# Three of VectorE's routing operations of a group of tokens folded into others

## The chip, the cores and the metric

The kernel runs on one core of one Trainium2 chip. The core's engines each follow their own list of instructions and wait for each other at semaphores: TensorE (PE, matmuls; PEld is its loading of weights), VectorE (DVE), ScalarE (ACT), GpSimd (POOL) and SyncE (SP, which here only issues transfers). 16 DMA engines move data between the main memory (HBM) and the on-chip memory (SBUF). Matmul results land in eight PSUM banks. The metric is the device time of one execution in microseconds, lower is better.

## The reference

Attention in chunks of 64 keys is followed by a mixture of experts in which each of 4608 tokens goes to one of 16 experts, picked in two steps (one of 4 groups by the largest of 4 logits, then one of the group's 4 experts):

```python
scores = scale * np.matmul(q_c, k_c.transpose(0, 1, 2, 4, 3))
scores = scores - np.max(scores, axis=-1, keepdims=True)
attn = np.exp(scores)
attn = attn / (np.sum(attn, axis=-1, keepdims=True) + 1e-09)
out = np.matmul(attn, v_c)
...
g_logits = x @ w_group
g_idx = np.argmax(g_logits, axis=1)
g_sm = softmax_of(g_logits)          # exp(l - max) / (sum + 1e-09)
g_w = g_sm[np.arange(N), g_idx]
for g in range(G):
    xg = x[g_idx == g]
    e_logits = xg @ w_expert[g]
    e_idx = np.argmax(e_logits, axis=1)
    e_w = the same softmax's value at e_idx
    for e in range(Eg):
        h = np.maximum(xg[e_idx == e] @ w1[g, e], 0.0)
        ye = h @ w2[g, e]
        out[those tokens] = (g_w * e_w)[:, None] * ye
```

`softmax_of` and the last lines are shortened here. B, H, S, D = 8, 8, 576, 64, so x has 4608 rows of 512, and each expert has F = 1024. All data is fp32.

## The kernel before

The 4608 tokens are 36 tiles of 128 (one token in each partition). An attention phase goes over the tiles in a software pipeline. In step t, SyncE loads queries, keys (`qk`) and values (`va`) ahead; TensorE makes the scores of tile t+1 (`stage_b`, L578); VectorE takes the maximum and subtracts it (`stage_sub`: `m` L586, `pr` L590); ScalarE exponentiates (`pr` L596); TensorE transposes (L602), ScalarE copies to `pT` (L604), TensorE multiplies by the values (L615); VectorE divides by the sums (`stage_norm`: `rc` L622 and L624, `x` L633); TensorE transposes `x` (L645), ScalarE copies it to `xT` (L646), and TensorE makes the router's logits (L665, L672), which ScalarE copies to `lg` (L673).

Four tiles are a group, so there are nine groups, 0 to 8. `route(g)` is VectorE's work on a group's 4 x 5 sets of 4 logits (one set over groups, four over the experts of each group): the maximum `mx` (L702), where it is (`one` L707), the differences `ls` (L709), the place of the maximum with ties going to the first (L713, L719, L721), the one-hot of 16 experts per token `oh` (L725), sums of the exponentials `sm` (L735; ScalarE exponentiates `ls` into `ex`, L691), the chosen group's sum (L738, L740), the added 1e-9 (L743), the reciprocal (L747), and the product, which is the token's weight (L750). `cum[:, g + 1]` is, by partition, how many tokens of groups 0 to g went to each expert: the sum of the group's four one-hots (L746) plus the count before (L748). `stage_e3(g)` turns counts and one-hots into each token's rank among its expert's tokens by matmuls (L763 to L768), `place(g)` and `one_scatter` turn that into row numbers (`pos`, L785 and L810), and GpSimd scatters the tokens' rows to those rows of `xs` in HBM (L801).

A Recorder takes all these instructions down in the order in which the code runs, works out the semaphore waits from the memory that each one reads and writes, and then plays each engine's list. `route` is a generator: each `yield` is a place where VectorE's list takes up attention work again (`more(n)` resumes it n times), so the two are interleaved by hand and each engine executes its list in order. The last tiles and the first steps of the first expert follow one string, TAIL. Then a loop over units of 128 or 256 tokens of one expert runs on TensorE with loaded weights (L1144, L1159), while VectorE and ScalarE split the next expert's fp32 weights into two parts. SBUF tiles are laid out one behind the other: the tile `cum` stands ahead of the weights' and the queries' buffers.

Of the kernel before, what the change touches and what calls it, by code (L numbers as in the profile page):

```python
# [10 lines left out]
F32 = mybir.dt.float32  # L11
F32R = mybir.dt.float32r
BF16 = mybir.dt.bfloat16
I32 = mybir.dt.int32
AF = mybir.ActivationFunctionType
ALU = mybir.AluOpType
AX = mybir.AxisListType
# [3 lines left out]
P = 128  # L21
# [7 lines left out]
E = G * EG  # L29
NT = N // P  # L30
NG = 4
RPE = N // P
NG0 = NT // NG
# [329 lines left out]
def moe_kernel(tc, qk, v, wgs, w1, w2, cst, out):  # L363
    nc = tc.nc
# [3 lines left out]
    with ExitStack() as ctx:  # L368
# [17 lines left out]
        cum = wpool.tile([P, NG0 + 1, E], BF16, name="cum")  # L386
# [96 lines left out]
        with ExitStack() as c1:  # L483
# [42 lines left out]
            R.vector.memset(cum[:, 0, :], 0.0)  # L526
# [165 lines left out]

            def route(g):
# [12 lines left out]
                one = rpool.tile([P, R5, 4], F32, name="one")  # L706
                V.tensor_tensor(out=by_t(one), in0=L, in1=by_t(mb), op=ALU.is_equal)  # L707
# [4 lines left out]
                io = cs[:, C_IOTA4:C_IOTA4 + 4].unsqueeze(1).broadcast_to([P, R5, 4])  # L712
                V.scalar_tensor_tensor(out=one, in0=one, scalar=-64.0, in1=io, op0=ALU.mult, op1=ALU.add)  # L713
                ex = rpool.tile([P, R5, 4], F32, name="ex")
                st["ex"] = ex, ls
# [8 lines left out]
                oh = rpool.tile([P, NG, 4, 4], BF16, name="oh")  # L724
# [7 lines left out]
                for i in range(NG):  # L732
# [6 lines left out]
                    elif i == 2:  # L739
                        V.tensor_reduce(out=sv[:, :, 1], in_=se, axis=AX.X, op=ALU.add)  # L740
                    else:
                        gt = rpool.tile([P, NG, 2], F32, name="gt")
                        V.tensor_scalar(out=gt, in0=sv[:, :, 0:2], scalar1=1e-9, scalar2=None, op0=ALU.add)  # L743
                    yield
                with nc.allow_low_precision(reason="a sum of four ones and zeros"):
                    V.tensor_reduce(out=cum[:, g + 1, :], in_=oh.rearrange("p t g e -> p (g e) t"), axis=AX.X, op=ALU.add)  # L746
                V.reciprocal(gt, gt)  # L747
                V.tensor_tensor(out=cum[:, g + 1, :], in0=cum[:, g + 1, :], in1=cum[:, g, :], op=ALU.add)  # L748
# [6 lines left out]
            def stage_e3(g):  # L755
# [8 lines left out]
                R.tensor.matmul(rk3, lhsT=ones, rhs=wide(cum[:, g, :], NG), start=False, stop=False)  # L764
# [5 lines left out]
                if g == GC:  # L770
                    n = rk[0:1, NG * E:NG * E + E]
                    R.tensor.matmul(n, lhsT=ones[:, 0:1], rhs=cum[:, g + 1, :], start=True, stop=True)
# [244 lines left out]
        with tc.tile_critical():  # L1017
            with nc.Block() as blk, nc.allow_low_precision(reason="sums of a whole number or of four ones, and zeros"):

                @blk.tensor  # L1020
                def _(pe):
# [163 lines left out]
                    pe.matmul(pxf[0][0:E, 0:1], lhsT=cum[:, NG0, :], rhs=ones[:, 0:1], start=False, stop=True).then_inc(S["TP"], 1)  # L1185
# [536 lines left out]
```

## Time and profile before

| | |
|---|---|
| three timed runs | 613.26, 613.39, 618.44 us (median 613.39) |
| the profiled execution, and its span | 618.42 us, 616.8 us |
| attention phase | to about 158 us of the span |
| busy in the span: PE, DVE, ACT, POOL | 579.8, 360.8, 263.3, 158.2 us |

The span runs from the first to the last instruction; 1.6 us of the execution lie outside it. The busy time of VectorE is spread over two phases that have different limits, so the profile is read by stretches of time.

### The profile page before, as it was taken

The page shows a single profiled execution, that of the slowest core. Times are in us where ns is not written, and L with a number is a line of the kernel's source. Part 1 is how long each engine was busy: PE and PEld are TensorE (multiplying, and loading weights), DVE is VectorE, ACT ScalarE, POOL GpSimd, SP SyncE. Part 2 cuts the span into 40 slices and gives each one's busy share as a digit, 9 for nine tenths or more (in the row PEclk, how much of TensorE's full clock was granted, in tenths as well). Part 3 has the DMA queues.
Part 4 walks back from the last instruction along what each step waited for, and adds up shares of the span by engine and source line. Part 5 has one row for each costly group of instructions (what it writes and reads, how often), then busy time and mean ns, then how long its engine had stood idle before and what let it go on. Part 6 is the DMA issues. An engine that isn't in the chain of part 4 may idle for free.

```text
span 616.8 us, 16000 instructions
## 1 busy us (share of the span) xinstructions
PE 579.8 (94%) x5711; PEld 498.9 (81%) x5712; DVE 360.8 (58%) x688; ACT 263.3 (43%) x367; POOL 158.2 (26%) x252
## 2 busy tenths in 40 slices
PE   7889979978998999999999999999999999999995
PEld 4666657756887989888889989889989988898984
DVE  4577869776767482136697474726326578763211
ACT  2455545756336241223685252626116355452111
POOL 0002314665403111212323312122111124321120
PEclk9899889997998999999999999999999999999999
DMA  7998997876549693118298763643613586921110
GB/s 280 422 312 277 352 366 240 243 228 207 163 146 395 240 330 109 39 30 296 103 348 311 261 245 121 221 153 113 236 51 123 208 323 223 331 105 64 34 44 24
DMA packets 43104, 128.27 MB, mean 208 GB/s; under 512 B 4590, under 2 KB 4974, under 8 KB 41136
## 3 DMA queue, kind: packets, MB, share of 16 engines
q1 hardware_dynamic: 32192, 93.93, 43.9%
q0 software_dynamic: 10864, 33.64, 15.5%
q8 instruction: 37, 0.61, 0.4%
q14 instruction: 11, 0.09, 0.1%
HBM read 106.40 MB, written 21.93 MB: 208 GB/s over the span
## 4 chain that ended last, share of the span: by engine, by line
PE 71%; DVE 11%; DMA 7%; issue 5%; POOL 2%; SPq 1%; ACT 1%; another core or an unknown queue 0%; DVEq 0%; POOLq 0%; ACTq 0%
PE banks L1159 28%; PE banks L1144 22%; PE banks L1128 4%; PE banks L615 2%; DVE x L633 2%; DVE pr L590 2%; DMA xgr<-xs 2%; DVE m L586 2%; DMA w1r<-in_moe_w_dram 2%; DMA qk<-in_qk_dram 2%; PE banks L471 2%; PE banks L602 2%; PE banks L1044 2%; PE banks L645 1%; PE banks L578 1%
## 5 line engine op out<-in xcount | busy, mean ns | idle before, releaser
L1144 PE MATMUL banks<-big,w1h 128*128 128x256 f32 x896 | 128.1, 283 | 1.4 <-issue 1.4
L1144 PEld LDWEIGHTS banks<-big,w1h 128*128 128x128 f32 x896 | 117.3, 192 | 2.9 <-issue 1.9
L1305 ACT ACTIVATE big<-banks 128x512 fp32r<-128x512 f32 x58 | 34.5, 596 | 158.9 <-PE banks L1144 126.0
L1159 PE MATMUL banks<-big,big 128*128 128x512 f32 x360 | 84.7, 393 | 0.0
L1635 POOL DMA_INDIRECT out_dram<-xl,io__154 x37 | 41.1, 1112 | 152.9 <-DVE xl L1371 144.4
L1159 PEld LDWEIGHTS banks<-big,big 128*128 128x128 f32 x360 | 66.5, 188 | 14.4 <-ACT big L1355 0.7
L1404 DVE SCALAR_TENSOR_TENSOR big<-banks,big 128x512 fp32r<-128x512 f32 x54 | 36.1, 687 | 64.3 <-ACT big L1305 62.0
L1159 PE MATMUL banks<-w2h,big 128*128 128x512 f32 x288 | 72.6, 399 | 0.2 <-ACT big L1305 0.2
L1144 PE MATMUL banks<-big,w1l 128*128 128x256 f32 x448 | 72.3, 283 | 0.6 <-DVE w1l L1381 0.6
L1381 DVE TENSOR_TENSOR w1l<-w1r,w1h 128x2048 fp32r<-128x2048 f32 x28 | 63.1, 2291 | 16.0 <-ACT w1h L1292 14.3
L1371 DVE TENSOR_SCALAR xl<-banks,io__154 128x512 f32<-128x512 f32 x33 | 24.7, 749 | 68.2 <-PE banks L1159 68.2
L1159 PEld LDWEIGHTS banks<-w2h,big 128*128 128x128 f32 x288 | 53.8, 190 | 12.2 <-ACT big L1305 0.9
L1144 PEld LDWEIGHTS banks<-big,w1l 128*128 128x128 f32 x448 | 61.9, 192 | 0.8 <-DVE w1l L1381 0.8
L1292 ACT CAST w1h<-w1r 128x2048 fp32r<-128x2048 f32 x28 | 52.2, 1903 | 7.8 <-DMA w1r<-in_moe_w_dram 6.0
L578 PE MATMUL banks<-qk 64*64 64x64 f32 x1152 | 27.8, 232 | 12.5 <-DMA qk<-in_qk_dram 3.5
L578 PEld LDWEIGHTS banks<-qk 64*64 64x64 f32 x1152 | 22.3, 141 | 20.8 <-DVE pr L590 4.5
L1385 DVE TENSOR_TENSOR w2l<-w2r,w2h 128x1024 fp32r<-128x1024 f32 x32 | 37.1, 1220 | 2.3 <-ACT w2h L1324 1.7
L1159 PE MATMUL banks<-w2l,big 128*128 128x512 f32 x144 | 35.6, 389 | 0.0
L604 ACT COPY pT<-banks 128x512 f32<-128x512 f32 x36 | 21.1, 586 | 33.6 <-PE banks L602 30.2
L615 PEld LDWEIGHTS banks<-va,pT 64*64 64x64 f32 x1152 | 21.4, 141 | 16.5 <-issue 4.8
L801 POOL DMA_INDIRECT xs<-x,pos x24 | 24.2, 1008 | 40.3 <-DVE pos L810 21.7
L1629 POOL COPY in__155<-xgr 128x2 int32<-128x2 int32 x22 | 10.7, 485 | 92.6 <-PE banks L1044 78.7
(223 smaller groups left out, 906.8 us busy)
## 6 DMA issues: line engine op xcount, KB each, us to landing
w1r<-in_moe_w_dram SPq DMA_DIRECT2D x30, 1024.0 KB
w2r<-in_moe_w_dram SPq DMA_DIRECT2D x30, 1024.0 KB
qk<-in_qk_dram SPq DMA_DIRECT2D x15, 1024.0 KB, 17.4
xgr<-xs POOLq DMA_DIRECT2D x38, 257.0 KB, 5.6
va<-in_v_dram SPq DMA_DIRECT2D x24, 390.0 KB
qk<-in_qk_dram SPq DMA_DIRECT2D x6, 512.0 KB, 8.7
w1r<-in_moe_w_dram POOLq DMA_DIRECT2D x2, 1024.0 KB, 9.4
w2r<-in_moe_w_dram POOLq DMA_DIRECT2D x2, 1024.0 KB, 8.2
```

The lines of the kernel that those rows point to most:

```text
L578: R.tensor.matmul(sc[cols, x, hp * CH:hp * CH + CH], lhsT=T[rows, 0, hp, cols], rhs=T[rows, 1, hp, cols], start=True, stop=True)
L615: R.tensor.matmul(o[cols, x, hp * W:hp * W + W], lhsT=pT[rows, hp, cols], rhs=v_at(2 * t + c)[rows, hp], start=True, stop=True)
L1128: m = pe.matmul(ph[n], a_[:, c, 0:P], w_[:, c, n * 512:(n + 1) * 512], start=(i == 0), stop=(i == 11))
L1144: m = pe.matmul(ph[f // 2][:, f % 2 * 256:f % 2 * 256 + 256], w_[:, c, f * P:(f + 1) * P], a_[:, c, :], start=(i == 0), stop=(i == 11))
L1159: m = pe.matmul(py[j], a_[:, f, half[j]], w_(b, f), start=(i == 0), stop=(i == 23))
L1292: lambda b, s, j: ac.copy(wt[b][0][:, s], w1r[j]), K1)
L1305: ac.activation(hth()[:, 2 * b:2 * b + 2, :], ph[b].rearrange("p (f t) -> p f t", f=2), AF.Relu).then_inc(S["Ha"], 1)
L1371: return ve.tensor_scalar(out=yb[:, j, :], in0=py[j], scalar1=io_[:, j, 1:2], scalar2=None, op0=ALU.mult)
L1381: lambda b, s, j: ve.tensor_sub(wt[b][1][:, s], w1r[j], wt[b][0][:, s].bitcast(F32)), K1, js)
L1385: m = ve.tensor_sub(wt[b][4 + 2 * j + i], w2r[j][:, 2 * i:2 * i + 2], wt[b][2 + j][:, 2 * i:2 * i + 2].bitcast(F32))
L1404: ve.scalar_tensor_tensor(out=htl()[:, 2 * b:2 * b + 2, :], in0=ph[b].rearrange("p (f t) -> p f t", f=2), scalar=0.0, in1=hth()[:, 2 * b:2 ...
L1635: gp.indirect_dma_start(out, bass.IndirectOffsetOnAxis(ap=io[:, j, 0:1].bitcast(I32), axis=0), yb[:, j, :], None, bounds_check=N - 1, oob_ ...
```

## The change

It takes three instructions of `route` out of VectorE's list for each of nine groups.

1. The place of the maximum. Before, one instruction marked where a logit equals the maximum and a second made of this -64 + index there and the index elsewhere. Now the second reads the differences `ls` directly: (ls == 0) times (index - 64), which is -64 + index at the maximum and 0 elsewhere.
2. The added 1e-9. `ex` has a fifth column that holds 1e-9 from the start, so the sum over five has it; the reciprocal reads the sum directly.
3. The running counts. Three tiles `ohs` of 5 x 16 take turns: row 0 is the count before the group, rows 1 to 4 are its one-hots. One sum over the five rows writes row 0 of the next tile. TensorE reads the counts there.

Two memsets of 128x20 are added at the program's start; the one that cleared `cum` now clears row 0 of the first tile. The three tiles take 480 bytes per partition where `cum` took 320, and so all tiles allocated behind them start 160 bytes further on.

```diff
@@ -383,7 +383,7 @@
         pos8 = wpool.tile([P, NG], I32, name="pos8")
-        cum = wpool.tile([P, NG0 + 1, E], BF16, name="cum")
+        ohs = [wpool.tile([P, NG + 1, E], BF16, name="oh%d" % i) for i in range(3)]
         ones = wpool.tile([P, P], BF16, name="ones")
...
@@ -523,7 +523,6 @@
             R.vector.memset(off[:, E:E1], 2.0 * P)
-            R.vector.memset(cum[:, 0, :], 0.0)
             wg = cpool.tile([P, 4, 32], F32, name="wg")
...
@@ -690,6 +689,11 @@
 
+            exs = [cpool.tile([P, 5 * NG, 5], F32, name="ex%d" % i) for i in range(2)]
+            for z in exs:
+                R.vector.memset(z[:, :, 4:5], 1e-9)
+            R.vector.memset(ohs[0][:, 0], 0.0)
+
             def route(g):
...
@@ -703,16 +707,15 @@
                 by_t = lambda z: z.rearrange("p (t r) j -> p t r j", r=5)
-                one = rpool.tile([P, R5, 4], F32, name="one")
-                V.tensor_tensor(out=by_t(one), in0=L, in1=by_t(mb), op=ALU.is_equal)
                 ls = rpool.tile([P, R5, 4], F32, name="ls")
...
 
-                io = cs[:, C_IOTA4:C_IOTA4 + 4].unsqueeze(1).broadcast_to([P, R5, 4])
-                V.scalar_tensor_tensor(out=one, in0=one, scalar=-64.0, in1=io, op0=ALU.mult, op1=ALU.add)
-                ex = rpool.tile([P, R5, 4], F32, name="ex")
-                st["ex"] = ex, ls
+                io = cs[:, C_I16:C_I16 + 4].unsqueeze(1).broadcast_to([P, R5, 4])
+                one = rpool.tile([P, R5, 4], F32, name="one")
+                V.scalar_tensor_tensor(out=one, in0=ls, scalar=0.0, in1=io, op0=ALU.is_equal, op1=ALU.mult)
+                ex = exs[g % 2]
+                st["ex"] = ex[:, :, 0:4], ls
                 if g >= GL - 1:
...
@@ -721,7 +724,8 @@
                 ov = one.rearrange("p (t r) j -> p t r j", r=5)
-                oh = rpool.tile([P, NG, 4, 4], BF16, name="oh")
+                oh5 = ohs[g % 3]
+                oh = oh5[:, 1:].rearrange("p t (g e) -> p t g e", g=4)
                 V.tensor_tensor(out=oh, in0=ov[:, :, 0, :].unsqueeze(3).broadcast_to([P, NG, 4, 4]),
...
@@ -740,12 +744,10 @@
                         gt = rpool.tile([P, NG, 2], F32, name="gt")
-                        V.tensor_scalar(out=gt, in0=sv[:, :, 0:2], scalar1=1e-9, scalar2=None, op0=ALU.add)
+                        V.reciprocal(gt, sv[:, :, 0:2])
                     yield
-                with nc.allow_low_precision(reason="a sum of four ones and zeros"):
-                    V.tensor_reduce(out=cum[:, g + 1, :], in_=oh.rearrange("p t g e -> p (g e) t"), axis=AX.X, op=ALU.add)
-                V.reciprocal(gt, gt)
-                V.tensor_tensor(out=cum[:, g + 1, :], in0=cum[:, g + 1, :], in1=cum[:, g, :], op=ALU.add)
+                with nc.allow_low_precision(reason="a sum of ones and zeros, at most 36"):
+                    V.tensor_reduce(out=ohs[(g + 1) % 3][:, 0], in_=oh5.rearrange("p t e -> p e t"), axis=AX.X, op=ALU.add)
                 yield
...
@@ -761,7 +763,7 @@
                 R.tensor.matmul(rk3, lhsT=one1, rhs=wide(cs[0:1, C_BASE:C_BASE + E], NG), start=True, stop=False)
-                R.tensor.matmul(rk3, lhsT=ones, rhs=wide(cum[:, g, :], NG), start=False, stop=False)
+                R.tensor.matmul(rk3, lhsT=ones, rhs=wide(ohs[g % 3][:, 0], NG), start=False, stop=False)
                 for i in range(NG - 1):
...
@@ -769,7 +771,7 @@
                     n = rk[0:1, NG * E:NG * E + E]
-                    R.tensor.matmul(n, lhsT=ones[:, 0:1], rhs=cum[:, g + 1, :], start=True, stop=True)
+                    R.tensor.matmul(n, lhsT=ones[:, 0:1], rhs=ohs[(g + 1) % 3][:, 0], start=True, stop=True)
                     cn = rpool.tile([1, E], F32, name="cn")
...
@@ -1182,7 +1184,7 @@
                     pe.matmul(pxf[0][0:E1, 0:2], lhsT=off, rhs=cs[0:1, C_PM:C_PM + 2], start=True, stop=False)
-                    pe.matmul(pxf[0][0:E, 0:1], lhsT=cum[:, NG0, :], rhs=ones[:, 0:1], start=False, stop=True).then_inc(S["TP"], 1)
+                    pe.matmul(pxf[0][0:E, 0:1], lhsT=ohs[NG0 % 3][:, 0], rhs=ones[:, 0:1], start=False, stop=True).then_inc(S["TP"], 1)
                     L1first(3)
...
```

VectorE's list, the first part of `route(0)` (from `mx`), with attention work (`rc`, the transformed `x`) in between. Before:

```order
L702 TENSOR_REDUCE mx_111<-lg_101 128x20
L707 TENSOR_TENSOR one_112<-lg_101,mx_111 128x80
L709 TENSOR_TENSOR ls_113<-lg_101,mx_111 128x80
L713 SCALAR_TENSOR_TENSOR one_112<-one_112,cs 128x80
L622 TENSOR_SCALAR rc_108<-banks 128x8
L719 TENSOR_REDUCE mx_111<-one_112 128x20
```

The same place now:

```order
L706 TENSOR_REDUCE mx_115<-lg_103 128x20
L711 TENSOR_TENSOR ls_116<-lg_103,mx_115 128x80
L716 SCALAR_TENSOR_TENSOR one_117<-ls_116,cs 128x80
L621 TENSOR_SCALAR rc_112<-banks 128x8
L722 TENSOR_REDUCE mx_115<-one_117 128x20
```

The row that wrote `one` from the logits is gone, and `ls` and the row that reads it stand next to each other, where one row stood between.

VectorE's list, the last part of `route(0)`, between `pr` of one tile and the division of another. Before:

```order
L590 TENSOR_TENSOR pr_106<-banks,m_105 128x2x4x64
L738 TENSOR_TENSOR se_117<-sm_116,one_112 128x16
L740 TENSOR_REDUCE sm_116<-se_117 128x4
L743 TENSOR_SCALAR gt_118<-sm_116 128x8
L746 TENSOR_REDUCE cum<-oh_115 128x16
L747 RECIPROCAL gt_118<-gt_118 128x8
L748 TENSOR_TENSOR cum<-cum 128x16
L622 TENSOR_SCALAR rc_110<-banks 128x8
L750 TENSOR_TENSOR xl<-gt_118 128x4
```

The same place now:

```order
L589 TENSOR_TENSOR pr_110<-banks,m_109 128x2x4x64
L742 TENSOR_TENSOR se_119<-sm_118,one_117 128x16
L744 TENSOR_REDUCE sm_118<-se_119 128x4
L747 RECIPROCAL gt_120<-sm_118 128x8
L750 TENSOR_REDUCE oh_65<-oh_64 128x16
L621 TENSOR_SCALAR rc_114<-banks 128x8
L752 TENSOR_TENSOR xl<-gt_120 128x4
```

Two rows less; the reciprocal follows the sum that it reads, and the sum over one-hots stands behind it.

TensorE's list, `stage_e3(0)` and the score matmuls behind it, with the semaphores that each row waits for (`ascalar`, `avector`: ScalarE's and VectorE's; `dq6`: a load of queries and keys). Before:

```order
L763 MATMUL banks<-cs,one_93 128x64 [waits ascalar]
L764 MATMUL banks<-cum,ones 128x64
L766 MATMUL banks<-oh_115,ones 128x48
L766 MATMUL banks<-oh_115,ones 128x32
L766 MATMUL banks<-oh_115,ones 128x16
L768 MATMUL banks<-oh_115,tri 128x64
L578 MATMUL banks<-qk_85 64x64 [waits dq6,avector]
```

The same place now:

```order
L765 MATMUL banks<-cs,one_95 128x64 [waits ascalar]
L766 MATMUL banks<-oh_64,ones 128x64
L768 MATMUL banks<-oh_64,ones 128x48
L768 MATMUL banks<-oh_64,ones 128x32
L768 MATMUL banks<-oh_64,ones 128x16
L770 MATMUL banks<-oh_64,tri 128x64
L577 MATMUL banks<-qk_87 64x64 [waits dq6,avector]
```

The counts come from a tile `oh`; the rows and what they wait for are the same.

## Rows read from the trace of the kernel before

**Rows 1.** The page: busy time by engine; tenths in 40 slices; the chain.
```profile
PE 579.8 (94%) x5711; PEld 498.9 (81%) x5712; DVE 360.8 (58%) x688; ACT 263.3 (43%) x367; POOL 158.2 (26%) x252
...
PE   7889979978998999999999999999999999999995
...
PEclk9899889997998999999999999999999999999999
...
PE 71%; DVE 11%; DMA 7%; issue 5%; POOL 2%; SPq 1%; ACT 1%; another core or an unknown queue 0%; DVEq 0%; POOLq 0%; ACTq 0%
```

**Rows 2.** Windows: each engine's busy us, granted clock, DMA share, GB/s.
```profile
16.00:36.00 20.00, 16.64 (x419) 12.98 (x420) 11.28 (x25) 9.37 (x19) 0.73 (x4) 0.91 1.02 420
56.00:66.00 10.00, 8.59 (x161) 6.06 (x161) 5.81 (x16) 3.89 (x8) 5.22 (x6) 0.83 1.02 368
86.00:96.00 10.00, 9.99 (x215) 7.14 (x215) 6.63 (x28) 4.97 (x11) 2.13 (x3) 0.85 0.92 312
146.00:156.00 10.00, 9.15 (x54) 7.19 (x55) 8.67 (x27) 5.37 (x11) 4.24 (x4) 0.66 0.60 203
196.00:206.00 10.00, 9.79 (x39) 7.87 (x39) 9.33 (x10) 5.18 (x5) 2.72 (x4) 0.89 1.00 394
206.00:400.00 194.00, 192.34 (x1204) 172.47 (x1203) 111.17 (x119) 83.41 (x92) 47.31 (x88) 1.00 0.57 198
400.00:617.00 217.00, 209.47 (x1308) 187.62 (x1307) 104.86 (x119) 77.28 (x88) 48.23 (x85) 0.99 0.41 146
```

**Rows 3.** Timeline of VectorE, group 1: start, us, line, operation.
```profile
50.75 0.23 DVE L702 TENSOR_REDUCE mx<-lg 128x20 f32<-128x80 f32 x1
51.02 0.24 DVE L707 TENSOR_TENSOR one<-lg,mx 128x80 f32<-128x80 f32 x1
51.18 0.23 DVE L709 TENSOR_TENSOR ls<-lg,mx 128x80 f32<-128x80 f32 x1
51.33 0.23 DVE L713 SCALAR_TENSOR_TENSOR one<-one,cs 128x80 f32<-128x80 f32 x1
51.48 0.16 DVE L622 TENSOR_SCALAR rc<-banks 128x8 f32<-128x8 f32 x1
...
52.78 0.68 DVE L586 TENSOR_REDUCE m<-banks 128x8 f32<-128x512 f32 x1
53.38 0.23 DVE L735 TENSOR_REDUCE sm<-ex 128x20 f32<-128x80 f32 x1
53.52 0.68 DVE L590 TENSOR_TENSOR pr<-banks,m 128x512 f32<-128x512 f32 x1
...
54.32 0.17 DVE L740 TENSOR_REDUCE sm<-se 128x4 f32<-128x16 f32 x1
54.53 0.17 DVE L743 TENSOR_SCALAR gt<-sm 128x8 f32<-128x8 f32 x1
54.61 0.26 DVE L746 TENSOR_REDUCE cum<-oh 128x16 bf16<-128x64 bf16 x1
54.79 0.19 DVE L747 RECIPROCAL gt<-gt 128x8 f32<-128x8 f32 x1
54.90 0.17 DVE L748 TENSOR_TENSOR cum<-cum 128x16 bf16<-128x16 bf16 x1
54.98 0.16 DVE L622 TENSOR_SCALAR rc<-banks 128x8 f32<-128x8 f32 x1
```

**Rows 4.** Timeline of VectorE: the first operation after groups 0 and 3.
```profile
41.92 0.17 DVE L622 TENSOR_SCALAR rc<-banks 128x8 f32<-128x8 f32 x1 [0.93 <-PE banks L615]
...
88.78 0.17 DVE L622 TENSOR_SCALAR rc<-banks 128x8 f32<-128x8 f32 x1 [1.62 <-PE banks L615]
```

**Rows 5.** The chain behind group 1: start, us, what.
```profile
57.46 0.63 ACT pr L596
58.09 2.37 another core or an unknown queue
```

**Rows 6.** Timeline of TensorE: the matmul ahead of 146 to 156.
```profile
146.85 0.96 PE L645 MATMUL banks<-cs,xl 128*128 128x128 f32 x4 [2.39 <-DVE xl L633]
```


## Prediction

> **What bounds the kernel now.** Start with the page [rows 1]. TensorE is busy in 94% of the span and makes 71% of the chain that ended last; VectorE makes 11% of it. The tenths in slices say where: TensorE is at 7 to 9 in the first ten slices, where the attention phase lies, and at 9 almost without a break from then on. The table of windows gives the same in numbers [rows 2]: from 206 us to the end TensorE is busy for 192.34 of 194 and 209.47 of 217 us, while VectorE is busy for 111.17 and 104.86. Routing is over by then, so whatever this change is worth has to come out of the first 158 us. There the limits alternate. In some stretches the transfers are the limit: from 16 to 36 us the DMA engines' share is 1.02 at 420 GB/s, from 56 to 66 us 1.02. In others it is VectorE: in the steps that hold a group's routing its operations stand one behind the other [rows 3], and the divided tile `x`, which TensorE needs next, waits in that row like everything else. The gain is therefore to be read from the starts of operations in such a row, not from their durations: one lasts 0.16 to 0.26 us, but the next often starts 0.08 to 0.18 us after it, because they overlap.
>
> **Part A, the place of the maximum.** The starts in group 1 [rows 3] go 50.75 (`mx`), 51.02 (`one`), 51.18 (`ls`), 51.33 (L713), 51.48 (the next tile's `rc`). An operation that reads what the one just ahead of it wrote starts 0.27 us behind it (`mx` to `one`); one that doesn't starts 0.15 to 0.16 us behind (`one` to `ls`, `ls` to L713, L713 to `rc`). Before, the instruction that reads `one` had `ls` between itself and its source, so nobody paid for that wait. The change takes this spacer away: `ls` starts 0.27 after `mx`, the instruction that reads it 0.27 later, `rc` 0.15 later, together 0.69 where 0.73 stood. **Part A gives 0.04 us a group**, not the 0.16 of a removed step. `ls` itself comes 0.16 us earlier, and ScalarE's `ex` with it, but the sum that reads `ex` starts only at 53.38, 2 us later, so this hides.
>
> **Parts B and C, the added 1e-9 and the counts.** From L740 (54.32) to the next `rc` (54.98) are 0.66 us, in steps of 0.21, 0.08, 0.18, 0.11 and 0.08 [rows 3]. Afterwards: L740 to the reciprocal 0.21, as it was to the addition, since each reads the sum just written; the reciprocal to the sum over one-hots 0.11, the step behind the reciprocal now; that sum to `rc` 0.18 for its 64 elements, plus 16 more. What an element costs follows from `m` (512 elements, step 0.60) and `sm` (80 elements, step 0.14): 0.46 / 432 = 0.001 us, so 16 make 0.02. The new total is 0.52, **0.14 us less a group**. The sum of the exponentials reads 100 instead of 80 elements: 0.02 more. No row shows a sum over five strided bf16 rows or a comparison with a multiplication in one instruction. For the first I take the bounds 0.18 (the step of the 64) and 0.26 (its whole duration), and 0.20, near the lower one, because the step and not the duration holds up the next; for the second 0.15, as the same kind of instruction on the same 80 elements takes at L713. At the upper bound a group gains 0.06 us less.
>
> **Sum.** 0.04 + 0.14 - 0.02 = 0.16 us a group, 1.4 us over nine groups. (The durations of the three removed, 0.24 + 0.17 + 0.17 = 0.58 us, make 5.2 us of busy time; that is what will be missing from VectorE's busy row, and it is not the gain.) Not all of the 1.4 lies on the path. Behind groups 0 and 3 VectorE stands idle for 0.93 and 1.62 us until TensorE has finished L615 [rows 4], so their parts B only lengthen that. Behind group 1 the chain runs into 2.37 us that belong to no engine [rows 5], in the stretch where DMA is full: what group 1 gains may be waited away there, and group 2 comes in the same crowded time. Groups 7 and 8 run beside the first expert's matmuls, which TensorE has to do in any case; its long wait there, 2.39 us at 146.85 [rows 6], isn't for routing. Groups 4, 5 and 6 are left: 0.5 us that I count in full, and of the 0.9 us of the others about a quarter. **Taken: 0.7 us, bounds 0 and 1.4.**
>
> The rest of the edits cost nothing. The added memsets stand at the program's start, ahead of the first scores, which TensorE makes behind 10 us of loading; without that cover they would cost some 0.2 us each, as any small operation here. The three tiles that take turns could bring a wait (a new count overwrites one that TensorE read for an earlier group), but that reading lies several tiles back, and the lists show the same waits on TensorE's rows as before. The queues of SyncE and GpSimd are not touched.
>
> **A rule that speaks another way.** In rows 3 a wait for the operation just ahead costs 0.11 to 0.12 us (0.27 against 0.15 to 0.16). The Trainium skill, page "VectorE: DVE Perf Modes", section "The DRAIN you can't avoid", says that semaphores between chained operations cost nothing extra, and the page's rules for kernel authors say to minimize the number of operations, not of semaphores. By that rule a removed operation saves its whole step, wherever it stood. The rows disagree with it for these short operations.
>
> **Where the profiled execution stands.** It took 618.42 us (616.8 of span and 1.6 around it). The three timed runs are 613.26, 613.39 and 618.44: two near 613.3, and one 5 us higher where the profiled one is too. Made against the profiled one, the sum is 617.7; against the median of 613.39 it is **612.7**, which I predict. Nothing in the change says which of the two levels the median of the next runs will be at.
>
> **Rivals.**
> 1. A removed operation saves its whole step (the rule above, as a mechanism here: VectorE would take up L716 0.15 us behind `ls`). Then part A gives 0.16 and a group 0.28: 2.5 us over nine, and if all of it were on the path, 610.9. For it: the steps of 0.15 in rows 3. Against it: the 0.27 between `mx` and `one`, 0.21 from L740 on.
> 2. Slower, by a loss of TensorE's clock. TensorE's granted clock fell in some stretches: 0.83 in 56 to 66, 0.85 in 86 to 96 and 0.66 in 146 to 156 us [rows 2], and each fall to the lower level of 1.2 GHz comes after TensorE stood still, as for 2.39 us ahead of the last [rows 6]. If VectorE gives its results earlier, TensorE runs ahead to the next wait for a transfer and stands there longer. One more stretch like the last costs 0.34 x 10 = 3.4 us, and its standing 1.7 us on top (2.39 less the 0.7 gained): 5.1 us, so 617.8. It decides once one wait becomes long enough to be followed by such a stretch. For it: the two levels of the runs lie 5.1 us apart, so something of that size comes and goes without any change. Against it: 0.16 us a group is little beside waits of 1.6 to 3 us.
> 3. The opposite: such a stretch goes, 612.7 - 5.1 = 607.6.
> 4. Slower, by the addresses. All large buffers start 160 bytes further on, no longer at multiples of 256. If transfers into them ran worse, the stretches with a full DMA share would stretch. The bound is from rows 2: per unit of share, 420 / 1.02 = 412 GB/s where values stream into tiles at odd places, and 394 / 1.00 where only weights flow, 4% apart in any direction; on the 40 us of 16 to 36, 56 to 66 and 196 to 206 that is 1.8 us: 614.5. Against it: the values' chunks of 3120 bytes start at all kinds of places already, and theirs is the higher rate. The Trainium skill, page "DMA: Bandwidth & Descriptors", section "How a descriptor splits into AXI transactions", says that a descriptor that doesn't start at a multiple of 256 bytes costs extra beats; the trace shows no such loss.
>
> **How the numbers follow.** The forecast, 612.0 to 613.4 with the gain between all and nothing: 0.58. Rival 1: 0.08. Rival 2 (or simply the upper level in most of the next runs): 0.22. Rival 3: 0.06. Rival 4: 0.06. The range from 610.5 to 618.2 holds all but rival 3 and tails on either side. 1%, 6.1 us, is about what a measurement of this kernel can tell from no change. Faster than 607.3 needs more than rival 3's middle: 0.04. Slower than 619.5 needs rival 2 on top of the upper level, or twice: 0.06. Within: 0.90.
>
> **What would show it.** In the changed trace: `ls` 0.27 us behind `mx` and the next operation 0.27, not 0.15, behind `ls` (part A and rival 1); 0.52 us from L740's place to the next `rc` (parts B and C); VectorE's busy time lower by about 5 us, and the end of the attention phase earlier by 1 us at the most. The forecast is wrong if the sum over five rows takes much more than 0.20 us to the next start, if a wait of TensorE appears at the first matmul that reads the counts, or if the granted clock falls below 1.00 in more or fewer places than the five windows of rows 2 that show it clearly.

## The result, and the profile after

The changed kernel takes **619.78 us** (median of 13 executions, 618.16 to 622.64); the kernel before, timed beside it, takes 613.19 (13 executions, 610.34 to 618.44). The ratio is 1.0112, 95% interval 1.0088 to 1.0137: slower by 1.1%, 6.6 us, where 612.7 was forecast. The profiled execution took 620.02 us. (The ratios, here and below, leave out executions more than 1.5% above the fastest of their kernel, which the medians include, so they are not quotients of the medians.)

The page of the changed kernel: busy time by engine, TensorE's and the clock's tenths, the chain.

```profile
PE 573.7 (93%) x5711; PEld 495.7 (80%) x5712; DVE 359.2 (58%) x663; ACT 264.2 (43%) x367; POOL 159.0 (26%) x252
...
PE   6789679989989999899969999999999999999995
...
PEclk9989999989989999999979999999999999999998
...
PE 66%; DVE 11%; DMA 10%; issue 5%; POOL 3%; SPq 1%; ACT 1%; POOLq 1%; DVEq 0%; ACTq 0%
```

Against [rows 1], two things stand out. DMA went from 7% of the chain to 10%, GpSimd from 2% to 3%. And TensorE, which stood at 9 in every slice of the second half but the last, has a 6 in its 21st slice (309 to 325 us), with a lower clock. That is some 150 us behind the end of all routing.

Windows of the changed kernel (busy us by engine, granted clock, DMA share, GB/s), the first line most of the attention phase, the last one the stretch of the new gap:

```profile
8.00:158.00 150.00, 124.63 (x2914) 97.45 (x2913) 109.34 (x354) 82.19 (x168) 49.74 (x57) 0.98 0.89 302
206.00:400.00 194.00, 186.67 (x1155) 167.06 (x1154) 108.71 (x116) 82.75 (x91) 45.93 (x86) 0.98 0.54 192
400.00:617.00 217.00, 210.74 (x1314) 188.71 (x1312) 105.92 (x121) 77.42 (x88) 48.08 (x85) 1.00 0.42 148
310.00:322.00 12.00, 6.24 (x30) 5.09 (x29) 5.00 (x6) 3.54 (x8) 2.22 (x5) 0.72 0.89 338
```

and those two stretches of the kernel before:

```profile
8.00:158.00 150.00, 126.65 (x2867) 97.05 (x2865) 109.74 (x375) 80.50 (x166) 48.58 (x56) 0.94 0.88 295
310.00:322.00 12.00, 12.00 (x63) 9.96 (x63) 11.41 (x11) 9.43 (x10) 2.87 (x2) 1.00 0.94 333
```

The attention phase is not worse: its mean granted clock is 0.98, where it was 0.94. From 206 to 400 us TensorE is busy for 186.67 us instead of 192.34 [rows 2], and all of that is lost between 310 and 322, where it works for 6.24 of 12 us and its clock is granted at 0.72.

The chain says what TensorE waited for there. Chain of the changed kernel, 290 to 322 us (start us, us, what):

```profile
299.52 5.41 DMA word<-xs
...
309.76 8.58 DMA xgr<-xs
```

`out_dram` (L1637) is GpSimd's scatter of a finished unit's rows. `word` (L1683) is a transfer of a single element that stands in for a second scatter in units of one tile or less (the kinds `k == 1` and `k == 0`), so that the semaphore counts the same. GpSimd then waits for both, copies the next unit's indices, and issues the gather `xgr` (L1626), which TensorE transposes (L1046). The timelines of the changed kernel show how long each step took. VectorE, GpSimd (without the other copies and the gather's second half), SyncE's queue and TensorE:

```profile
294.74 0.74 DVE L1379 SCALAR_TENSOR_TENSOR xl<-banks,io__154,xl 64x512 f32<-64x512 f32 x1
296.31 4.49 DVE L1383 TENSOR_TENSOR w1l<-w1r,w1h 128x2048 fp32r<-128x2048 f32 x2 [0.83 <-issue]
...
296.40 3.11 POOL L1637 DMA_INDIRECT out_dram<-xl,io__154  x1 [2.15 <-DVE xl L1379]
299.52 0.56 POOL L1683 DMA_DIRECT2D word<-xs  x1
305.08 0.74 POOL L1631 COPY io__154<-in__155 128x2 int32<-128x2 int32 x1 [5.01 <-DMA word<-xs]
308.99 0.58 POOL L1626 DMA_DIRECT2D xgr<-xs  x1 [0.78 <-POOL in__155 L1632]
...
298.77 2.58 SPq L459 DMA_DIRECT2D w1r<-in_moe_w_dram  x2
...
316.92 0.75 PE L1046 MATMUL banks<-identr,xgr 128*128 128x128 f32 x4 [5.04 <-DMA xgr<-xs]
318.38 0.75 PE L1046 MATMUL banks<-identr,xgr 128*128 128x128 f32 x4 [0.71 <-DMA xgr<-xs]
```

The same place in the kernel before, which came there 6 us later:

```profile
300.64 0.74 DVE L1377 SCALAR_TENSOR_TENSOR xl<-banks,io__154,xl 64x512 f32<-64x512 f32 x1
302.30 4.53 DVE L1381 TENSOR_TENSOR w1l<-w1r,w1h 128x2048 fp32r<-128x2048 f32 x2 [0.91 <-issue]
...
302.30 1.03 POOL L1635 DMA_INDIRECT out_dram<-xl,io__154  x1 [2.21 <-DVE xl L1377]
303.34 0.55 POOL L1681 DMA_DIRECT2D word<-xs  x1
305.32 1.55 POOL L1629 COPY io__154<-in__155 128x2 int32<-128x2 int32 x1 [1.42 <-DMA word<-xs]
308.35 0.58 POOL L1624 DMA_DIRECT2D xgr<-xs  x1 [0.77 <-POOL in__155 L1630]
...
304.80 2.58 SPq L459 DMA_DIRECT2D w1r<-in_moe_w_dram  x2
...
317.43 0.89 PE L1044 MATMUL banks<-identr,xgr 128*128 128x128 f32 x8
```

Read both from VectorE's product into `xl`, which GpSimd scatters. GpSimd starts the scatter 1.66 us behind that product's start in both kernels. VectorE starts its next work, the first of two subtractions into `w1l` (the low part of the next expert's weights, some 2.3 us each), 1.66 us behind it before and 1.57 us now. So both started at 302.30 before; now VectorE is 0.09 us ahead. The scatter takes 1.03 us before and 3.11 now, and is over 0.9 us after the first subtraction. The same subtraction's end also lets SyncE load the next weights (298.77, 304.80). Before, `word` was issued ahead of that load and GpSimd stood for 1.42 us; now it is issued 0.75 us behind it and GpSimd stands for 5.01. The gather is issued 12.59 us behind the scatter's start (308.99), 6.05 before (308.35): of these 6.54 us, 2.08 are the longer scatter, 3.59 the longer wait, and the rest is in GpSimd's copies of indices. It also takes longer to land: its two halves 7.9 and 8.6 us, where they took 5.0 and 5.1. Before, TensorE was still busy when they had landed; now it stands for 5.04 + 0.71 us. Its next matmuls run at the lower of the clock's two levels: 0.75 us for four transposes, where before eight took 0.89.

The sum fits. From the start of this scatter to the end of the span are 616.8 - 302.30 = 314.5 us before, 618.4 - 296.40 = 322.0 now: 7.5 us more. TensorE's standing is 5.75 of it, the slower transposes 1.50 - 0.89 = 0.61, and by the same timelines the four matmuls of L1062 and the eight by `w2h` (L1161) that follow take 1.07 and 2.92 us instead of 0.62 and 2.17: 1.20. Together 7.56. (The two profiled executions lie only 1.6 us apart, 618.42 and 620.02, because that of the kernel before was 5.9 us later at this scatter.)

### The profile page after: what moved, and what is told of

The parts are those of the page before. It is cut to its first block, busy times and chain, and to the rows that moved or that the text cites. A ratio compares the mean times of both kernels' runs of the same rounds, so it can differ in the third digit from the quotient of the medians.

```text
span 618.4 us, 15975 instructions
## 1 busy us (share of the span) xinstructions
PE 573.7 (93%) x5711; PEld 495.7 (80%) x5712; DVE 359.2 (58%) x663; ACT 264.2 (43%) x367; POOL 159.0 (26%) x252
## 4 chain that ended last, share of the span: by engine, by line
PE 66%; DVE 11%; DMA 10%; issue 5%; POOL 3%; SPq 1%; ACT 1%; POOLq 1%; DVEq 0%; ACTq 0%
PE banks L1161 29%; PE banks L1146 22%; DMA xgr<-xs 4%; PE banks L1130 4%; DVE m L585 2%; DVE pr L589 2%; DMA cs<-in_cst_dram 2%; DVE x L632 2%; PE banks L1046 2%; PE banks L614 2%; DMA out_dram<-xl,io__154 1%; PE banks L1092 1%; PE banks L577 1%; PE banks L601 1%; POOL xs L803 1%
## 5 line engine op out<-in xcount | busy, mean ns | idle before, releaser
L1161 PE MATMUL banks<-big,big 128*128 128x512 f32 x360 | 84.6, 393 | 0.0
L1637 POOL DMA_INDIRECT out_dram<-xl,io__154 x37 | 42.0, 1135 | 152.1 <-DVE xl L1373 143.9
L1161 PEld LDWEIGHTS banks<-big,big 128*128 128x128 f32 x360 | 66.5, 188 | 14.2 <-ACT big L1357 0.7
L1161 PE MATMUL banks<-w2h,big 128*128 128x512 f32 x288 | 71.7, 396 | 0.0
L1161 PEld LDWEIGHTS banks<-w2h,big 128*128 128x128 f32 x288 | 53.9, 190 | 11.2
L577 PE MATMUL banks<-qk 64*64 64x64 f32 x1152 | 25.9, 229 | 14.0 <-DMA qk<-in_qk_dram 4.2
L577 PEld LDWEIGHTS banks<-qk 64*64 64x64 f32 x1152 | 21.0, 139 | 20.8 <-DVE pr L589 6.7
L1161 PE MATMUL banks<-w2l,big 128*128 128x512 f32 x144 | 35.6, 389 | 0.0
L614 PE MATMUL banks<-va,pT 64*64 64x65 f32 x1152 | 25.6, 227 | 9.8 <-DVE m L585 2.9
```

The costliest lines, as they stand in the source:

```text
L577: R.tensor.matmul(sc[cols, x, hp * CH:hp * CH + CH], lhsT=T[rows, 0, hp, cols], rhs=T[rows, 1, hp, cols], start=True, stop=True)
L614: R.tensor.matmul(o[cols, x, hp * W:hp * W + W], lhsT=pT[rows, hp, cols], rhs=v_at(2 * t + c)[rows, hp], start=True, stop=True)
L1161: m = pe.matmul(py[j], a_[:, f, half[j]], w_(b, f), start=(i == 0), stop=(i == 23))
L1637: gp.indirect_dma_start(out, bass.IndirectOffsetOnAxis(ap=io[:, j, 0:1].bitcast(I32), axis=0), yb[:, j, :], None, bounds_check=N - 1, oob_ ...
```

## Experiments

The theory: **a race for a fraction of a microsecond between VectorE and GpSimd, 150 us behind the change, is decided the other way** since VectorE's list is 25 instructions shorter ahead of that place and one branch in the loop costs it 0.08 us less. (The views leave branches out; by the trace's records it is 0.27 us from the start of one branch ahead of the subtraction to the next record before, and 0.19 now, the other ten steps being the same within 0.005.) Its rivals: the addresses, moved by 160 bytes; a longer attention phase; the folded operations themselves.

One number tells whether a profiled execution lost the race, whatever its attention phase did: the time from that scatter's start to the end of the span. The table gives it for every profile, with the ratio to the kernel before, timed beside it on the same chip. Those medians of before were 612.16 us beside the first four runs, 610.17 beside the next four, 615.71 beside the last four.

| run | median us | ratio, 95% interval | scatter starts, lasts | scatter to end |
|---|---|---|---|---|
| before | 613.19 | | 302.30, 1.03 | 314.5 |
| after | 619.78 | 1.0112, 1.0088 to 1.0137 | 296.40, 3.11 | 322.0 |
| before again | 619.49 (one) | | 303.59, 1.04 | 314.2 |
| after + 25 memsets | 611.40 | 1.0003, 0.9967 to 1.0038 | 297.43, 1.04 | 314.6 |
| before, addresses | 612.65 | 0.9999, 0.9958 to 1.0040 | 297.82, 1.04 | 314.1 |
| after, VectorE later | 614.76 | 1.0008, 0.9963 to 1.0053 | 303.66, 1.03 | 313.5 |
| before, GpSimd later | 617.68 | 1.0106, 1.0075 to 1.0137 | 297.20, 3.08 | 321.6 |
| part A alone | 613.03 | 1.0047, 1.0005 to 1.0088 | 300.43, 1.04 | 314.3 |
| part B alone | 610.43 | 0.9989, 0.9953 to 1.0025 | 301.63, 1.04 | 314.3 |
| part C alone | 615.91 | 1.0069, 1.0025 to 1.0112 | 301.12, 1.04 | 314.4 |
| part C again | 616.94 | 1.0011, 0.9976 to 1.0046 | 298.56, 1.03 | 314.2 |
| part C + 9 memsets | 617.26 | 1.0029, 0.9998 to 1.0061 | 303.87, 1.03 | 313.5 |
| after, halves | 616.29 | 1.0011, 0.9971 to 1.0052 | 299.59, 2.05 | 314.7 |
| after, loads later | 618.31 | 1.0057, 1.0019 to 1.0094 | 296.03, 3.12 | 317.2 |

**The kernel before, once more** (no edit).

> The kernel before, once more, for a second profile of it. Race theory: in the expert phase, VectorE's first subtraction into w1l (L1381) in the unit after the two quarter units and GpSimd's scatter (L1635) start within 0.1 us of each other; in the changed kernel VectorE is 0.09 us ahead and GpSimd's scatter takes 3.11 us instead of 1.03. In every execution of the kernel before the scatter should take about 1.0 us, the gather after it should land before TensorE needs it, and no wait of TensorE of more than 1 us for xgr should stand in the rows. Clock theory (the attention phase's low-clock stretches alone make the difference): a time near 613 with fewer or shorter low stretches than the profile at 618.42 had, and the scatter says nothing.

The scatter took 1.04 us, `word` kept GpSimd for 1.42, and TensorE did not wait for this gather. This execution took 619.49 us, as long as the changed kernel's, and yet the race was won: its scatter started only at 303.59 us. So a single time says nothing here. What differs between these two executions of one kernel is the way to that scatter (over all fourteen profiles it takes 296 to 304 us); what differs between won and lost is the way from it (some 314 and 322).

**The changed kernel with VectorE's list as long as before.**

```diff
             one1 = cpool.tile([1, P], F32, name="one1")
+            for i in range(25):
+                R.vector.memset(one1[:, i:i + 1], 1.0)
             R.vector.memset(one1, 1.0)
```

> The changed kernel with 25 more memsets of one element on VectorE at its very start, so that its list has as many instructions as before. Code-place theory (VectorE's list is shorter, a taken branch of the loop costs 0.08 us less there, and that decides who is first, VectorE's subtraction or GpSimd's scatter): the scatter in that unit is back at 1.0 us, TensorE's wait of 5.0 us for the gather is gone, and the time is 611 to 615. Address theory (buffers moved by 160 bytes make the operations or transfers of the loop slower or faster): addresses are the changed kernel's, so it stays at 618 to 621, the scatter at 3.1 us. Theory that the folded operations themselves delay the attention phase: 620 to 622.

The 6.6 us are gone, with more instructions and every folded operation in place. VectorE and GpSimd of this kernel:

```profile
297.42 4.53 DVE L1385 TENSOR_TENSOR w1l<-w1r,w1h 128x2048 fp32r<-128x2048 f32 x2 [0.91 <-issue]
...
297.43 1.04 POOL L1639 DMA_INDIRECT out_dram<-xl,io__154  x1 [2.15 <-DVE xl L1381]
```

The subtraction's start is within 0.01 us of the scatter's again, and the branch at 0.27 us. That excludes the addresses and the folded operations as causes: both are the changed kernel's here.

**The kernel before with the changed addresses.**

```diff
         cum = wpool.tile([P, NG0 + 1, E], BF16, name="cum")
+        wpool.tile([P, 80], BF16, name="spare")
```

> The kernel before with 160 bytes per partition left free behind cum, so that the buffers behind it lie where the changed kernel has them. Code-place theory: VectorE's list is unchanged, the scatter takes 1.0 us, and the time is that of the kernel before, 611 to 615. Address theory: 618 to 621, with the scatter at 3.1 us or another operation of the loop slower.

No difference: 0.9999. The addresses are out from the other side too.

**The changed kernel with VectorE held back at the place itself** (units of `k == 0`, one tile; the expectation calls the kind a half).

```diff
                             with ve.Else():
+                                for i in range(4):
+                                    W("TB", 1)
                                 prep1(code)
```

> The changed kernel with four waits on VectorE that are long fulfilled, put ahead of the subtraction into w1l in units of the one-token-half kind, nothing else. Race theory: these delay VectorE by 0.1 to 0.4 us there, GpSimd's scatter starts first and takes 1.0 us, the gather lands in time, and the time is 611 to 615, although the list of VectorE ahead of that place is the changed kernel's. Theory that the scatter's 3.11 us is a consequence and not the cause: the scatter stays at 3 us and the time at 618 to 621.

It came 0.10 us behind GpSimd (303.76 against 303.66), the scatter took 1.03 us, and 313.5 us follow it, as with the race won. The ratio, 1.0008, says the same; since the median is 2.6 us above that of before, the weight of this run lies on the 313.5. No instruction ahead of the place was changed, and so the order of the two is the cause, not the place in the code as such.

**The kernel before with GpSimd held back.**

```diff
+                        W("Y", 2 * u + 3)
+                        for i in range(4):
+                            W("TB", 1)
                         scatter(2 * u + 2, 0)
```

> The kernel before with four waits on GpSimd that are long fulfilled, put between the wait for VectorE's product and the scatter of a unit, nothing else. Race theory: GpSimd comes 0.1 to 0.4 us later to its scatter, VectorE's first subtraction into w1l is ahead, the scatter of that unit takes 2.5 to 3.2 us instead of 1.03, the small transfer behind it lands 5 us later than it should, TensorE waits about 5 us for the gather, and the time is 617 to 621, with none of the routing change in it. Theory that the place in the code alone costs something, not the order of the two: 611 to 615.

This makes the loss without any routing change: 1.0106 against 1.0112. (The waits stand in every unit. The next unit's scatter, at 311.66 us, takes 3.08 us; there it takes 2.32 in the kernel before too.) VectorE, GpSimd and TensorE of this kernel:

```profile
297.08 4.50 DVE L1381 TENSOR_TENSOR w1l<-w1r,w1h 128x2048 fp32r<-128x2048 f32 x2 [0.91 <-issue]
...
297.20 3.08 POOL L1635 DMA_INDIRECT out_dram<-xl,io__154  x1 [2.68 <-issue]
...
316.95 0.75 PE L1044 MATMUL banks<-identr,xgr 128*128 128x128 f32 x4 [4.49 <-DMA xgr<-xs]
```

**Each part alone**, on the kernel before: A (the place of the maximum, 9 instructions fewer on VectorE), B (the 1e-9 in the sums, 7 fewer), C (the counts in the one-hots, 9 fewer). The edits are those lines of the diff above that belong to the part; C moves the addresses as well.

> The kernel before with the new place of the maximum alone: 9 instructions fewer on VectorE. Code-place and race theory: all or nothing; either the branch before the subtraction into w1l costs what it did (the scatter 1.0 us, 610 to 615), or it is cheaper (the scatter 2.5 to 3.2 us, 617 to 621); nothing in between. Theory that each part brings its share of the 6.6 us: 614 to 616.

> The kernel before with the 1e-9 as a fifth element of the sums alone: 7 instructions fewer on VectorE in all. Code-place and race theory: all or nothing as for the other parts, with the scatter at 1.0 us and 610 to 615, or at 2.5 to 3.2 us and 617 to 621. Theory of shares: 614 to 616.

> The kernel before with the running counts as a fifth row of the one-hot alone: 9 instructions fewer on VectorE, and the buffers behind it moved by 160 bytes. Code-place and race theory: VectorE's list is as long as with the new place of the maximum alone, so the subtraction and the scatter stand to each other as there; scatter and time like that run's. Theory of shares, or of addresses: 614 to 616, or 618 to 621, whatever that run gives.

All three profiles have the race won, with 314.3, 314.3 and 314.4 us behind the scatter; the branch is at 0.265 us in each, still dear. So in these profiles no part brings a share of the loss, and of what was tried only all 25 together pass the point. The expected two levels did not come out in the times, though: A and C measured 1.0047 and 1.0069, between them. In the profiled executions the way from the scatter on is that of before, so what was lost there lies ahead of it. So part C was run once more:

> The kernel with the running counts as a fifth row alone, unchanged, a second time: was its 1.007 the kernel's or that of the executions? Theory that the granted clock's stretches in the attention phase fall out differently from execution to execution, and a program's small shifts in time move them at most by chance: 0.997 to 1.004, with the scatter at 1.0 us and from the scatter to the end 314 us again. Theory that this kernel has an attention phase of its own that is 4 us longer: 1.004 to 1.011 again.

and with nine memsets more:

```diff
+            for i in range(9):
+                R.vector.memset(one1[:, i:i + 1], 1.0)
             R.vector.memset(one1, 1.0)
```

> The same kernel with 9 more memsets of one element at VectorE's start, so that its list is as long as before. Theory that the attention phase alone made the 1.007: what the run beside it gives, within 0.004. Theory that VectorE's shorter list cost it (in some executions the scatter is held after all, since the margin is 0.008 us): 0.997 to 1.003, below the run beside it by 0.004 or more.

The same kernel gave 1.0069 in one set of executions and 1.0011 in the next; its two scatters start at 301.12 and 298.56 us. The nine memsets made it no faster (1.0029; its interval overlaps with both), which speaks against the list's length as the cause. What varies is the attention phase. Some of it may go with the granted clock: from 8 to 158 us that is 0.98 in the changed kernel's profile, 0.94 and 0.87 in the two of the kernel before, whose scatters start at 296.40, 302.30 and 303.59. Not all of it does: in part C's two profiles it is 0.93 and 0.92, and they lie 2.6 us apart; with the 25 memsets it is 0.91, and the scatter starts at 297.43. The cause of this spread stays open. A ratio of up to 1.007 from one set of executions therefore proves no difference between kernels here; part A's 1.0047 was not repeated and stays open in that sense.

**What the 7.5 us are made of.** Two edits of the changed kernel keep VectorE ahead (1.58 us behind the product, GpSimd 1.66). The first makes each subtraction two of half the size:

```diff
+                    def half1(b, s, j):
+                        for i in range(K1):
+                            n = s.start + i
+                            m = ve.tensor_sub(wt[b][1][:, n:n + 1], w1r[j][:, i:i + 1], wt[b][0][:, n:n + 1].bitcast(F32))
+                        return m
...
                             with ve.Else():
-                                prep1(code)
+                                prep1h(code)
```

> The changed kernel with each subtraction into w1l in units of the one-half-tile kind written as two of half the size. VectorE still comes 0.09 us before GpSimd. Theory that the scatter stands until the running VectorE operation ends: the first one is over after about 1.2 us instead of 2.3, the scatter takes about 2.0 us instead of 3.1, the small transfer behind it is issued before the first weights' load, and the time is 611 to 615 with no wait of TensorE for the gather. Theory that the scatter stands as long as VectorE subtracts at all: 3 us or more, 617 to 621.

GpSimd, SyncE's queue and TensorE of this kernel:

```profile
299.59 2.05 POOL L1646 DMA_INDIRECT out_dram<-xl,io__154  x1 [2.66 <-DVE xl L1379]
301.64 0.56 POOL L1692 DMA_DIRECT2D word<-xs  x1
304.66 0.19 POOL L1640 COPY io__154<-in__155 128x2 int32<-128x2 int32 x1 [2.45 <-DMA word<-xs]
...
302.04 2.65 SPq L459 DMA_DIRECT2D w1r<-in_moe_w_dram  x2
...
316.13 0.54 PE L1046 MATMUL banks<-identr,xgr 128*128 128x128 f32 x4 [0.78 <-DMA xgr<-xs]
```

The scatter takes 2.05 us: it ends 0.9 us behind the half that was running when it started, and is held no longer, although VectorE goes on subtracting. `word` is issued 0.40 us ahead of the load, keeps GpSimd for 2.45 us, and TensorE waits for 0.78: 1.0011, no loss that can be measured.

The second leaves the subtractions whole, but signals both buffers free only after the second:

```diff
+                                    for j in range(NP):
+                                        W("P1a", NP * code + (j + 1))
+                                        k = slice(K1 * j, K1 * j + K1)
+                                        m = ve.tensor_sub(wt[b][1][:, k], w1r[j], wt[b][0][:, k].bitcast(F32))
+                                    m.then_inc(S["P1d"], NP)
```

> The changed kernel in which, in units of that kind, VectorE tells that it is done with both halves of the weights' buffer after the second subtraction instead of after each: both loads start 2.2 us later, the scatter is still held. Theory that the small transfer's place behind the weights' load does the harm, not the 2 us of the scatter: the scatter stays at 3.1 us, the small transfer lands in 1.4 to 2 us instead of 5.4, TensorE waits under 1 us for the gather, 611 to 616. Theory that the 2 us of the scatter alone make the gather late: TensorE waits 2 to 5 us, 616 to 621.

GpSimd, SyncE's queue and TensorE of this kernel:

```profile
296.03 3.12 POOL L1647 DMA_INDIRECT out_dram<-xl,io__154  x1 [1.75 <-DVE xl L1379]
299.15 0.55 POOL L1693 DMA_DIRECT2D word<-xs  x1
301.14 0.19 POOL L1641 COPY io__154<-in__155 128x2 int32<-128x2 int32 x1 [1.43 <-DMA word<-xs]
303.08 1.24 POOL L1641 COPY in__155<-xgr 128x2 int32<-128x2 int32 x1 [1.64 <-issue]
304.27 1.20 POOL L1642 COPY in__155<-xgr 128x2 f32<-128x2 f32 x1
...
300.61 1.05 SPq L459 DMA_DIRECT2D w1r<-in_moe_w_dram  x2
...
312.03 0.53 PE L1046 MATMUL banks<-identr,xgr 128*128 128x128 f32 x4 [0.50 <-DMA xgr<-xs]
313.84 0.54 PE L1046 MATMUL banks<-identr,xgr 128*128 128x128 f32 x4 [1.27 <-DMA xgr<-xs]
```

Neither expectation holds in full. The scatter is held for as long as in the changed kernel, and `word` lands in time, 1.43 us of waiting as in the kernel before; but TensorE still waits for 0.50 + 1.27 us, and the ratio is 1.0057 (1.0019 to 1.0094), by itself within the spread just named. From the scatter to the end are 317.2 us: 2.7 more than in the kernel before, 4.8 less than in the changed kernel. So **most of the loss, 4.8 us, goes when `word` and the loads change places; of the 2.7 that stay, the scatter's 2 us are a part at the most**. They are not a clean second term. Both loads come later in this run, and GpSimd's next two copies of indices were held as well, beside VectorE's subtractions into `w2l` from 303.06 us on: 1.24 and 1.20 us, where each took 0.19 in the kernel before. That puts the gather off by as much again as the scatter did: it is issued 10.21 us behind the scatter's start, 6.05 before.

No version beats both kernels. The edits that mend the order bring the changed kernel to the time of the one before, and no further than the intervals of 0.4 to 0.5% can tell.

## Why the prediction was wrong, point by point

- **Part A** was right. VectorE of the changed kernel, group 1, against [rows 3]:

```profile
51.05 0.24 DVE L706 TENSOR_REDUCE mx<-lg 128x20 f32<-128x80 f32 x1
51.32 0.24 DVE L711 TENSOR_TENSOR ls<-lg,mx 128x80 f32<-128x80 f32 x1
51.59 0.24 DVE L716 SCALAR_TENSOR_TENSOR one<-ls,cs 128x80 f32<-128x80 f32 x1
51.75 0.16 DVE L621 TENSOR_SCALAR rc<-banks 128x8 f32<-128x8 f32 x1
...
53.65 0.25 DVE L739 TENSOR_REDUCE sm<-ex 128x20 f32<-128x100 f32 x1
53.82 0.68 DVE L589 TENSOR_TENSOR pr<-banks,m 128x512 f32<-128x512 f32 x1
...
54.61 0.17 DVE L744 TENSOR_REDUCE sm<-se 128x4 f32<-128x16 f32 x1
54.82 0.20 DVE L747 RECIPROCAL gt<-sm 128x8 f32<-128x8 f32 x1
54.94 0.24 DVE L750 TENSOR_REDUCE oh<-oh 128x16 bf16<-128x80 bf16 x1
55.11 0.15 DVE L621 TENSOR_SCALAR rc<-banks 128x8 f32<-128x8 f32 x1
```

  `ls` starts 0.27 us behind `mx`, L716 0.27 behind `ls`, `rc` 0.16 behind that: 0.70, where 0.69 was forecast and 0.73 stood. Rival 1, a whole step saved, falls with it: the wait for the operation just ahead is there.
- **Parts B and C** were right: 0.50 us from L744 to `rc` (0.52 forecast, 0.66 before). The sum over five strided rows has a step of 0.17 us, under the 0.18 to 0.26 that were allowed. The sum over 100 elements costs 0.17 instead of 0.14, so 0.03, not 0.02. Together 0.03 + 0.16 - 0.03 = 0.16 us a group, as forecast.
- **Busy time lower by about 5 us** was wrong: it fell by 1.6 (360.8 to 359.2) with 25 instructions fewer, though the sum of all durations in the trace fell by 4.7. The row counts overlapping operations once, so it falls by what the steps shrink (0.16 x 9 = 1.4), not by the removed durations. The text had made that very distinction for the gain and then forgot it for the row.
- **The gain of 0.7 us** could be neither confirmed nor refuted. With the order mended the ratio is 1.0003 (0.9967 to 1.0038) and 1.0008 (0.9963 to 1.0053); 0.7 us would be 0.9989.
- **Rival 4**, the addresses, fell: 0.9999 with the addresses alone. **Rival 2** named a time near the measured one, 617.8, by a mechanism in the wrong phase: a lower clock in attention. In the profiles the attention phase of the changed kernel had less of it than that of the kernel before (0.98, 0.94). The new stretch at a lower clock, 0.72 from 310 to 322 us, comes with TensorE's standing of 5.04 us for the gather, which no part of the prediction has; that the time came out near rival 2's is luck.
- **The step that failed** is in the first part: that "whatever this change is worth has to come out of the first 158 us". With it fell "The rest of the edits cost nothing" and "The queues of SyncE and GpSimd are not touched". Their lists are indeed the same; but VectorE's list is shorter ahead of the loop, VectorE came 0.08 us earlier to one subtraction there, and that made GpSimd's scatter 2 us longer, its wait 3.6 us longer and its gather 6.5 us later. The prediction had looked for VectorE's neighbours only where routing is. It could have listed the places of the expert phase where two engines start within 0.1 us of each other: the trace of before shows 302.30 for both. The Trainium skill, page "SBUF — State Buffer", section "Who interferes with whom", would have named the pair: a VectorE instruction with two inputs in SBUF contends with a GpSimd instruction that reads SBUF, and the order of issue decides who is blocked. The runs agree: the subtraction reads `w1r` and `w1h`, the scatter its indices `io_`, and 0.09 us decide between 1.03 and 3.11 us. No page or row would have given the 0.08 us of the branch in advance, so the change was a draw with two outcomes, one of them 7.5 us worse.

## What to carry to other kernels

Before an edit that only shortens one engine's list, look through the rest of the program, not only the edited stretch, for two engines that start within some 0.1 us of each other on a path with little slack; price the other order, and make it safe (here four waits that are already fulfilled, or two halves of one operation, mended the loss). Where a time moves by more than the edit can explain, cut the span at one event behind the edit and compare both pieces: here the way from one scatter to the end was 313.5 to 314.7 us with the race won or the operation halved, and some 322 with it lost (317.2 with the loads held back), while the way to it varied by 8 us from profile to profile, and by 2.6 us in one and the same kernel. And put a kernel's length back with idle instructions before blaming what was edited.

## What the runs showed of the hardware

- An indirect scatter issued by GpSimd took 1.03 to 1.04 us beside VectorE's 2.3 us subtraction where both started within 0.01 us (nine profiles), and 3.08 to 3.12 where VectorE was 0.08 to 0.12 us ahead (three); it ended 0.9 us after that operation, whole or halved (3.11, 2.05). Two copies of indices were held too (1.24 and 1.20 us instead of 0.19). A plain transfer by GpSimd was not: `word` took 0.56 us at 299.52 beside the second subtraction, which ran from 298.5 to 300.8 us.
- A hold need not cost much: one unit later the scatter takes 2.33 us in the kernel before too (at 316.73 us in its second profile), `word` then keeps GpSimd for 5.85 us, and TensorE waits for the gather behind it for only 0.21 us. What counts is whether the next gather has that much time.
- A transfer of one element issued 0.75 us behind the first of two 1 MB loads kept its waiter for 5.0 us, one issued 0.40 us ahead of the first for 2.45, one issued 1.46 us ahead for 1.42.
- From one branch of VectorE's loop to the next record it is 0.19 us in the changed kernel, 0.265 with 16 to 18 instructions more ahead of it, 0.27 with 25 more. The Trainium skill, page "Runtime: NRT & Kernel Launch", section "Instruction fetch mechanics", says that a taken branch can wait for its target to be fetched; that this is the reason is argued, since no run here shows the fetching.
